# Experts' first pass on 32 rows in four column groups, x gathered in half rows, a fourth home for expert weights

## The chip, the cores and the metric

The kernel runs on one core of a Trainium2 chip. The metric is the device time of one execution in microseconds (us). Times of a kernel are given as the median of several runs; one further execution is profiled, and every duration below comes from that one.

## The reference

Three layers in float32, the last one with float64 weights as inputs:

- Attention over 2 x 8 heads, 768 positions, head width 64: a local window of 16 and block summaries of 32 keys. Its output is x, 1536 rows of 512.
- A mixture of experts with one expert per row and a skip: only rows whose skip score is positive are computed.

```python
do_compute = x @ w_skip > 0
e_idx = np.argmax(xc @ w_gate, axis=1)          # xc: the rows that are computed
for e in range(8):
    h = np.maximum(xc[mask_e] @ w1[e], 0.0)     # 512 -> 1024
    y[mask_e] = gate_w * (h @ w2[e])            # 1024 -> 512
out[do_compute] = xc + y                        # other rows: x as it is
```

- A dense layer on all rows: `h = x @ w_in` (512 to 2048), `g = h * tanh(softplus(h))`, `g @ w_out` (2048 to 512).

Worked through with the reference's own inputs, the routing sends 23, 131, 179, 9, 3, 60, 13 and 10 rows to experts 0 to 7; 1108 rows skip.

## The kernel before

Three stages follow one another on the core. Attention ends at about 100 us of the profiled span, the expert stage runs to about 215 us, and the dense layer fills the rest.

**Routing.** At the end of attention DVE and PE build, per expert, a list of row numbers: `choices` compares each row's rank with `pos` (192 ranks), `pick` turns this by small matmuls into the lists, `id_lists` writes `idl` (half 0: the first 128 ranks, of which 64 are used; half 1: ranks 64 to 191), `counts` writes the number of rows of each expert to `cnti`, and `gate_lists` makes the gate weights. `idle` issues matmuls whose result nobody reads.

**Gathers.** POOL fetches by indirect DMA the first 64 rows of every expert into `xtile[e]` and rows 64 to 191 into three spare tiles `xsb`, 12 gathers one behind the other. All five engines then load nine counts into registers (`load_count`).

**An iteration e of the expert loop.** `g1_pair` multiplies 64 rows by w1[e]: the array is used as two column groups of 64, one for each half of the 1024 hidden columns, 512 moving columns each, over four slices `kk` of the depth. Between the second and the third slice PE transposes the previous expert's hidden layer (`flip`, four blocks of 128), behind the fourth it transposes the next expert's rows (`flip_small`). Then `g2_pair` multiplies the previous expert's hidden layer by w2[e-1], again in two column groups. `If(regs[e] > 64)` runs `whole(e)`, a second pass on 128 more rows with the full array. DVE closes expert e-1 (`close_small`: two passes over 64 x 512), POOL scatters the result to `xd` in DRAM, and DVE converts slices of the dense layer's float64 weights (`go_conv`, six DVE instructions each, ten slices in this stage by `CONVS`).

**Weights.** One expert has 4.19 MB, eight loads of 512 KB on SP's queue. There are three homes: `fwp` for experts 0, 3 and 6, `stg` and `rawp` for 1, 4 and 7, `ring2` for 2 and 5. The first three experts' weights are loaded during attention. Loads of expert e+2 are issued in iteration e, behind `g2_pair(e-1)`, once their home is free. Every engine takes its instructions in the written order (`manual_schedule`).

**Into the dense layer.** Behind the loop come the last `g2_pair`, part of a conversion, the last `close_small` and its scatter. `x_first` loads rows of `xd` back, PE transposes them (`x_turn`, L1313) and the dense layer begins. Its matmuls (L1135, L1384) fill PE to the end.

Of the kernel before, what the change touches and what calls it, by code (L numbers as in the profile page):

```python
# [20 lines left out]
P = 128  # L21
# [7 lines left out]
def kernel(  # L29
# [37 lines left out]
    HT = P // 2  # L67
    CUT = HT + P
# [23 lines left out]
    gtl = const.tile([P, 2, E], F32, name="gtl")  # L92
    tri = const.tile([P, P], BF16, name="tri")
# [74 lines left out]
    def room(key):  # L168
# [5 lines left out]
        if e % 3 == 1:  # L174
            if nm == "w1":
                return stg.tile([P, 2, 512], F32, tag="stg", name="raw")
            return spool[0].tile([P, 2, 512], F32, tag="raw", name="raw")
        if kk % 2 == 0:
            if e % 3 == 0:
                open_[nm] = big((0 if nm == "w1" else 2) + kk // 2)  # L180
            else:
                t = ring2.tile([P, 2, 2, DM], F32R, tag="w2", name="wb")
                open_[nm] = t.rearrange("p a b d -> p (a b) d").bitcast(F32)
# [26 lines left out]
    ring = []  # L210

    make_identity(nc, ident)

    def setup_routing():
# [10 lines left out]
        nc.gpsimd.iota(idp[:, :, 0], pattern=[[P, TT]], base=-IDB, channel_multiplier=0,  # L225
                       allow_small_or_imprecise_dtypes=True)
        nc.gpsimd.iota(idp[:, :, 1], pattern=[[0, TT]], base=0, channel_multiplier=1,
                       allow_small_or_imprecise_dtypes=True)
        nc.gpsimd.iota(pos, pattern=[[1, CUT]], base=0, channel_multiplier=0,
                       allow_small_or_imprecise_dtypes=True)  # L230
        nc.gpsimd.memset(one, 1.0)
# [40 lines left out]
    pos = win.tile([P, CUT], BF16, name="pos")  # L272
# [149 lines left out]
    def idle(lhs, rhs, n, cols):  # L422
        t = ps.tile([P, 512], F32, tag="x", name="idle")[:, 0:cols]
# [168 lines left out]
    def choices(t0, t1):  # L592
        for t in range(t0, t1):
            sels[t] = win.tile([P, CUT], BF16, name=f"sel{t}")
            nc.vector.tensor_scalar(out=sels[t], in0=pos, scalar1=rkf[:, t:t + 1], scalar2=None, op0=ALU.is_equal)
# [10 lines left out]
    def pick(t0, t1, pieces):  # L606
# [3 lines left out]
        mv = mvs.pop((t0, w))  # L610
        lp = ps.tile([P, 2, w, E], F32, tag="tr", name="lp")
        for half in range(2):
            for t in range(t0, t1):
                nc.tensor.matmul(lp[:, half].rearrange("p w e -> p (w e)"), sels[t][:, half * HT:half * HT + P],
# [5 lines left out]
    def id_lists(t0, t1):  # L620
        lpv = pick(t0, t1, idp)
        if t0 == 0:
            nc.vector.tensor_scalar(out=early, in0=lpv, scalar1=float(IDB) / 2, scalar2=None, op0=ALU.add)
        else:
            nc.vector.tensor_tensor(out=early, in0=early, in1=lpv, op=ALU.add)
            nc.vector.tensor_tensor(out=idl, in0=early[:, :, :, 0], in1=early[:, :, :, 1], op=ALU.add)
# [91 lines left out]
    FEED_AT = dict(zip((6, 7, 8, 9, 10, 11, 12, 13, 14, 16, 17, 18, 19, 20), (1, 1, 1, 1, 1, 2, 1, 2, 2, 2, 2, 2, 2, 2)))  # L718
# [201 lines left out]
    id_lists(0, TB)  # L920
# [42 lines left out]
    idle(ident, ident, 2, P)  # L963
# [22 lines left out]
    rows = [ring[0].tile([P, 4, DM], F32, tag="w1", name="xr") for _ in range(E // 4)]  # L986
    xtile = [rows[e // 4][:, e % 4, :] for e in range(E)]
    for t in xtile[:2]:
        nc.gpsimd.memset(t, 0.0)
    for t in (xsb[0], xtile[2], xsb[1], xtile[3], xsb[2], *xtile[4:]):  # L990
        nc.vector.memset(t, 0.0)

    def fetch(idx, t):
        ins = nc.gpsimd.indirect_dma_start(
            out=t, out_offset=None, in_=xd[:, :],
            in_offset=bass.IndirectOffsetOnAxis(ap=idx, axis=0), bounds_check=NT - 1, oob_is_err=False)
# [3 lines left out]
    def store(idx, t):  # L1000
        apart("store", nc.gpsimd.indirect_dma_start(  # L1001
            out=xd[:, :], out_offset=bass.IndirectOffsetOnAxis(ap=idx, axis=0),
            in_=t, in_offset=None, bounds_check=NT - 1, oob_is_err=False), ("store", "fetch"))

    def flip(src, tag):
        pt = mps.tile([P, KD, P], F32, tag=tag, name="pt", bufs=1)
        for c in range(KD):
            nc.tensor.transpose(out=pt[:, c, :], in_=src[:, c * P:(c + 1) * P], identity=ident)  # L1008
        return pt

    def flip_small(src):
        pt = mps.tile([P, KD, HT], F32, tag="xt", name="pt", bufs=1)
        for c in range(KD):
            nc.tensor.transpose(out=pt[:, c, :], in_=src[0:HT, c * P:(c + 1) * P], identity=ident[0:HT, 0:HT])
# [7 lines left out]
    def relu(hp_, tag="hr"):  # L1022
        hr = mo.tile([P, 512], F32, tag=tag, name="hr", bufs=(3 if tag == "hr" else 2))
# [3 lines left out]
    def g1_pair(e, xT, hp_, lo, hi):  # L1027
        for kk in range(lo, hi):
            w = raws["w1", e, kk].rearrange("p a b -> p (a b)")
            for h in range(2):  # L1030
                nc.tensor.matmul(hp_[h * HT:(h + 1) * HT], xT[:, kk, :], w[:, h * 512:(h + 1) * 512],  # L1031
                                 start=(kk == 0), stop=(kk == KD - 1))

    def g2_pair(e, hT, yp, lo=0, hi=KD):
        for c in range(lo, hi):
            for h in range(2):
                nc.tensor.matmul(yp[h * HT:(h + 1) * HT], hT[:, c, h * HT:(h + 1) * HT],  # L1037
                                 raws["w2", e, 2 * h + c // 2][:, c % 2, :], start=(c == 0), stop=(c == KD - 1))
# [467 lines left out]
```

## Time and profile before

| | us |
|---|---|
| median of 3 runs | 507.59 |
| lowest, highest | 506.62, 512.57 |
| profiled execution | 501.91 |
| its span | 500.2 |

The span is the time from the first to the last instruction of the profiled execution; 1.7 us lie around it. In the profile an instruction is named by engine, line and operation, with the tile that it writes and those that it reads. PE is the matrix engine (TensorE), PEld its weight loads, DVE the vector engine, ACT the scalar engine, POOL the engine that issues the gathers, SP the one that issues the other transfers. A float32 matmul shows as two records. A column `x16` counts records. "Landing" is the time from the issue of a transfer until its data is there.

### The profile page before, as it was taken

The numbers are of one execution on the slowest core, as the hardware profiler recorded it, in microseconds if no ns is written. First come the engines' busy times: TensorE is split into PE (matmuls) and PEld (weight loads), VectorE is DVE, ScalarE is ACT, GpSimd is POOL, SyncE is SP. The second block draws the span as 40 slices with busy tenths as digits, with TensorE's granted clock in tenths as the row PEclk, the third lists the DMA queues.
The fourth block names the chain that finished last, engine by engine and source line by source line (L and its number), as shares of the span: only waits on it lengthen the run. The fifth ranks groups of instructions, "written<-read, shape, count | busy, mean of one in ns | idle before, by whom it ended". The sixth has DMA issues, their size and how long they took to land.

```text
span 500.2 us, 8558 instructions
## 1 busy us (share of the span) xinstructions
PE 476.3 (95%) x3262; PEld 365.2 (73%) x3262; DVE 327.8 (66%) x628; ACT 264.5 (53%) x382; POOL 76.5 (15%) x114
## 2 busy tenths in 40 slices
PE   8999998978999999979999999999999999999996
PEld 7777776743434332358989898989898989898985
DVE  4578889740070897634888889887888887453535
ACT  3586772202111121226967778676767676767570
POOL 3368943072020230100000000000000000000000
PEclk9999998959999999999999999999999999999999
DMA  8999999956829399850412121212121000030003
GB/s 202 231 220 245 260 333 354 396 195 229 325 68 370 89 379 397 298 203 12 157 42 86 42 86 42 85 51 76 53 74 54 31 1 2 0 127 0 1 0 126
DMA packets 43695, 74.32 MB, mean 149 GB/s; under 512 B 18863, under 2 KB 18863, under 8 KB 43361
## 3 DMA queue, kind: packets, MB, share of 16 engines
q1 hardware_dynamic: 42080, 71.96, 45.2%
q0 software_dynamic: 1568, 1.76, 1.2%
q8 instruction: 28, 0.46, 0.4%
q14 instruction: 19, 0.15, 0.1%
HBM read 68.80 MB, written 7.86 MB: 153 GB/s over the span
## 4 chain that ended last, share of the span: by engine, by line
PE 54%; DMA 9%; issue 6%; DVE 4%; ACT 2%; POOL 1%; POOLq 0%; DVEq 0%
PE acc L1384 24%; PE hp L1135 23%; DMA xd<-yo,idl 5%; DMA xs<-xd,idl 4%; PE hp L1062 1%; PE yp L1067 1%; PE ptx L1313 1%; PE hp L1031 1%; PE yp L1037 1%; POOL xd L1001 1%; DVE big L1376 1%; DVE big L1365 1%; DMA big<-xd 1%; DVE big L1353 0%; PE pt L1008 0%
## 5 line engine op out<-in xcount | busy, mean ns | idle before, releaser
L1135 PE MATMUL hp<-xt,wi 128*128 128x384 f32 x768 | 140.1, 336 | 2.1 <-ACT xt L1318 1.4
L1135 PEld LDWEIGHTS hp<-xt,wi 128*128 128x128 f32 x768 | 134.5, 188 | 5.3 <-ACT xt L1318 1.9
L1384 PE MATMUL acc<-wo,big 128*128 128x512 f32 x576 | 138.3, 392 | 0.0
L1384 PEld LDWEIGHTS acc<-wo,big 128*128 128x128 f32 x576 | 107.2, 188 | 20.9
L1350 ACT ACTIVATE big<-hp 128x384 f32<-128x384 f32 x64 | 31.3, 492 | 65.7 <-PE hp L1135 65.6
L1365 DVE TENSOR_TENSOR big<-big 128x768 f32<-128x768 f32 x32 | 30.6, 957 | 33.6 <-ACT big L1361 33.6
L1353 DVE COPY big<-hp 128x384 f32<-128x384 f32 x64 | 35.5, 555 | 23.3 <-ACT big L1350 23.3
L1361 ACT ACT_TABLE_LOAD x32 | 41.1, 1283 | 0.6
L1350 ACT ACT_TABLE_LOAD x31 | 39.8, 1283 | 0.6
L1376 DVE TENSOR_TENSOR big<-big 128x768 fp32r<-128x768 f32 x32 | 30.7, 959 | 3.1
L1055 DVE SCALAR_TENSOR_TENSOR yo<-yp,gtl,xs 128x512 f32<-128x512 f32 x2 | 1.5, 752 | 45.8 <-PE yp L1067 45.8
L1361 ACT ACTIVATE big<-big,turn 128x768 f32<-128x768 f32 x32 | 30.0, 939 | 0.4
L370 ACT COPY hT<-pt 128x512 f32<-128x512 f32 x10 | 5.9, 586 | 45.9 <-PE pt L1008 45.9
L1357 ACT ACTIVATE big<-big 128x768 f32<-128x768 f32 x32 | 27.1, 847 | 1.0
L450 DVE TENSOR_REDUCE mx<-sps 128x4 f32<-128x480 f32 x24 | 15.7, 653 | 15.8 <-PE sps L442 15.7
L138 DVE SCALAR_TENSOR_TENSOR cv<-raw,cv 128x512 uint32<-128x512 uint32 x32 | 22.2, 695 | 1.1
L141 DVE SCALAR_TENSOR_TENSOR cv<-raw,cv 128x512 uint32<-128x512 uint32 x32 | 21.9, 684 | 0.3
L1001 POOL DMA_INDIRECT xd<-yo,idl x10 | 10.3, 1030 | 70.8 <-DVE yo L1055 44.5
L1024 ACT ACTIVATE hr<-hp 128x512 f32<-128x512 f32 x12 | 7.2, 598 | 25.9 <-PE hp L1031 15.9
L464 ACT ACTIVATE pts<-tp 120x512 f32<-120x512 f32 x23 | 13.7, 596 | 12.4 <-PE tp L459 11.4
L1373 DVE CAST big<-big 128x768 fp32r<-128x768 f32 x32 | 17.9, 560 | 3.0
L477 PE MATMUL xp<-vw,pts 120*64 120x65 f32 x384 | 17.4, 232 | 2.3 <-issue 1.9
(199 smaller groups left out, 647.8 us busy)
## 6 DMA issues: line engine op xcount, KB each, us to landing
big<-in_moe_w_dram SPq DMA_DIRECT2D x24, 512.0 KB, 7.5
raw<-in_moe_w_dram SPq DMA_DIRECT2D x24, 512.0 KB, 7.0
wb<-in_moe_w_dram SPq DMA_DIRECT2D x16, 512.0 KB, 7.5
raw<-in_moe_w_in_dram SPq DMA_DIRECT2D x16, 512.0 KB, 3.6
raw<-in_moe_w_out_dram SPq DMA_DIRECT2D x16, 512.0 KB, 3.4
kr<-in_k_dram SPq DMA_DIRECT2D x16, 192.0 KB, 4.8
qr<-in_q_dram SPq DMA_DIRECT2D x16, 192.0 KB, 5.3
xd<-xb SPq DMA_DIRECT2D x6, 512.0 KB, 6.8
```

The lines of the kernel that those rows point to most:

```text
L138: nc.vector.scalar_tensor_tensor(out=tu, in0=low, scalar=29, in1=tu, op0=ALU.logical_shift_right, op1=ALU.bitwise_or)
L141: nc.vector.scalar_tensor_tensor(out=tu, in0=high, scalar=0xC0000000, in1=tu, op0=ALU.bitwise_and, op1=ALU.bitwise_or)
L477: nc.tensor.matmul(xv[qs, c, h, :], pt[:, j, qs], vw[:, 4 * g + 2 * c + half, h, VP - D - 1:VP], start=True, stop=True)
L1135: last_up[0] = nc.tensor.matmul(ps_, l(a), r(b_), start=(kk == 0 and n == 0), stop=(kk == KD - 1 and n == 2))
L1350: nc.scalar.activation(out=part(ds[n], half), in_=hps[n, half], func=AF.Sigmoid, scale=-1.0)
L1353: nc.vector.tensor_copy(part(us[n], half), hps.pop((n, half)))
L1357: nc.scalar.activation(out=d, in_=d, func=AF.Arctan)
L1361: nc.scalar.activation(out=d, in_=d, func=AF.Sin, scale=-2.0, bias=turn2)
L1365: nc.vector.tensor_tensor(out=u, in0=u, in1=part(ds[n], half), op=ALU.mult)
L1373: nc.vector.tensor_copy(g_part(n, 0, half), part(us[n], half))
L1376: nc.vector.tensor_tensor(out=g_part(n, 1, half), in0=part(us[n], half), in1=g_part(n, 0, half).bitcast(F32), op=ALU.subtract)
L1384: nc.tensor.matmul(accs[t], g[:, a, t * P:(t + 1) * P], wo[f // 2][:, b_, f % 2, :], start=(n in FIRST and m == 0), stop=(n in LAST and m ...
```

## The change

- The first pass takes 32 rows, not 64. The array is used as four column groups of 32: four groups of 256 hidden columns in the first product (`g1_quad`), two halves of the depth times two halves of the columns in the second (`g2_quad`). A row of x is gathered as two half rows of 256, so that `xtile[e]` is 128 x 256: partitions 0 to 63 hold rows 0 to 31, partitions 64 to 127 rows 32 to 63. `flip` then has two blocks.
- Rows 32 to 63 are a new conditional pass `next_rows` (count over 32), the rest is `whole` as before (count over 64).
- The two halves of the lists are made one after the other, with more `idle` matmuls between; row numbers of half 0 are those of half rows.
- A fourth home: four `ring` tiles, filled with expert 3's weights as soon as the first gathers have landed. Homes are A B C D A B C A. Expert 4's loads are issued in iteration 1, those of 5, 6 and 7 in iterations 2, 3 and 5.
- PE loads expert e's count inside iteration e; the other engines load all nine ahead of the loop.
- Conversions stand ahead of `close_small` (`AHEAD`), between the two conditionals (`BETWEEN`) and at the end of an iteration (`BEHIND`), nine in the loop as before. Two loads of the first three experts' weights move from the attention loop to the remainder behind it (`FEED_AT`).

```diff
-        if e % 3 == 1:
+        home = "ABCDABCA"[e]
+        if home == "B":
...
-    idle(ident, ident, 2, P)
+    idle(ident, ident, 8, P)
...
-    choices(t0, TT)
-    id_lists(t0, TT)
-    idle(ident, ident, 5, P)
+    choices(t0, TT, 0, 1)
+    id_lists(t0, TT, 0)
+    idle(ident, ident, 9, P)
     counts()
+    choices(t0, TT, 1, 2)
+    id_lists(t0, TT, 1)
+    nc.vector.tensor_copy(idn, idl[HT:P, 0, :])
+    idle(ident, ident, 6, P)
     run(rest, 9)
     gate_lists(0, TT)
-    idle(ident, ident, 4, P)
+    idle(ident, ident, 6, P)
...
+    def g1_quad(e, xT, hp_, at, lo, hi):
         for kk in range(lo, hi):
+            n, c = divmod(kk, 2)
             w = raws["w1", e, kk].rearrange("p a b -> p (a b)")
+            for j in range(4):
+                nc.tensor.matmul(hp_[j * TQ:(j + 1) * TQ], xT[:, c, at + n * TQ:at + (n + 1) * TQ],
+                                 w[:, j * HM:(j + 1) * HM], start=(kk == 0), stop=(kk == KD - 1))
+
+    def g2_quad(e, hT, yp, lo=0, hi=2):
+        for i in range(lo, hi):
+            for c in range(2):
+                for h in range(2):
+                    j = 2 * h + i
+                    for n in range(2):
+                        nc.tensor.matmul(yp[(2 * h + n) * TQ:(2 * h + n + 1) * TQ], hT[:, c, j * TQ:(j + 1) * TQ],
+                                         raws["w2", e, j][:, c, n * HM:(n + 1) * HM],
+                                         start=(i == 0 and c == 0), stop=(i == 1 and c == 1))
...
+    def next_rows(e, xT):
+        hp_ = acc_h("hw", HM)
+        g1_quad(e, xT, hp_, HT, 0, KD)
+        hT = drawn(flip(relu(hp_, "yo"), "ht"), "hn", nc.scalar, 3)
+        yp = acc_h("hw", HM)
+        g2_quad(e, hT, yp)
+        close_small(e, yp, HT)
...
+    for nm in ("w1", "w2"):
+        load_expert(3, nm)
+    for eng in engs[1:]:
+        load_counts(range(E + 1), (eng,))
...
+    FOLLOWS = {1: 4, 2: 5, 3: 6, 5: 7}
+    AHEAD = (0, 1, 1, 0, 0, 0, 0, 0)
+    BETWEEN = (0, 2, 2, 0, 0, 0, 0, 0)
+    BEHIND = (0, 0, 0, 1, 1, 0, 1, 0)
...
     for e in range(E):
+        hp_ = acc_h(n=HM)
+        g1_quad(e, xT, hp_, 0, 0, 2)
+        load_counts((e,) if e + 1 < E else (e, E), (ENG.PE,))
         if e:
+            hT = drawn(flip(hr, "ht"), "hn", nc.scalar, 3)
+        g1_quad(e, xT, hp_, 0, 2, KD)
+        hr = relu(hp_, "hq")
+        own_xT = xT
         if e + 1 < E:
+            xT = drawn(flip(xtile[e + 1], "xt"), "xT", nc.scalar)
+        convert(AHEAD[e])
         if e:
+            yp = acc_y(HM)
+            g2_quad(e - 1, hT, yp, 0, 1)
             if e == E - 1:
+                hT_last = drawn(flip(hr, "ht"), "hn", nc.scalar, 3)
+            g2_quad(e - 1, hT, yp, 1, 2)
+            close_small(e - 1, yp)
+            if e in FOLLOWS:
+                for nm in ("w1", "w2"):
+                    load_expert(FOLLOWS[e], nm)
+        if BETWEEN[e]:
+            with tc.If(count(e) > TQ):
+                next_rows(e, own_xT)
+            convert(BETWEEN[e])
+            with tc.If(count(e) > HT):
+                whole(e, spare_of(e))
+        else:
+            with tc.If(count(e) > TQ):
+                next_rows(e, own_xT)
+                with tc.If(count(e) > HT):
+                    whole(e, spare_of(e))
```

## Rows read from the trace of the kernel before

**Rows 1.** The page's 40 equal slices of the span: PE's busy tenths and its granted clock.
```profile
PE   8999998978999999979999999999999999999996
PEclk9999998959999999999999999999999999999999
```

**Rows 2.** Busy time by window: stretch, its length, engines, granted clock, DMA share, GB/s.
```profile
core 0: us, PE busy (x) PEld busy (x) DVE busy (x) ACT busy (x) POOL busy (x), PEclk, DMA share, GB/s
107.40:113.20 5.80, 5.80 (x14) 1.71 (x16) 0.43 (x1) 0.00 (x0) 4.32 (x5) 0.50 1.01 362
123.25:139.40 16.15, 15.47 (x48) 7.21 (x46) 0.00 (x0) 2.95 (x5) 0.00 (x0) 1.00 0.73 261
181.20:189.90 8.70, 8.37 (x40) 2.86 (x40) 7.88 (x15) 1.45 (x3) 2.05 (x2) 1.00 1.03 408
```

**Rows 3.** Timeline of PE over iteration 5: start, duration, line, operation, shape, records, idle before.
```profile
181.24 1.94 PE L1031 MATMUL hp<-wb,xT 128*64 128x512 f32 x8 [0.34 <-DMA wb<-in_moe_w_dram]
183.11 0.66 PE L1008 MATMUL pt<-ident,hr 128*128 128x128 f32 x4
183.69 1.94 PE L1031 MATMUL hp<-wb,xT 128*64 128x512 f32 x8
185.56 0.46 PE L1014 MATMUL pt<-ident,xr 64*128 64x64 f32 x4
185.96 3.65 PE L1037 MATMUL yp<-raw,hT 128*64 128x512 f32 x16
189.95 1.51 PE L1031 MATMUL hp<-big,xT 128*64 128x512 f32 x6 [0.34 <-PEq L1252]
```

**Rows 4.** Timeline of PE in attention: matmuls on 32-column groups and on 64x64 quarters.
```profile
91.63 0.41 PE L512 MATMUL end<-xt,wg 128*32 128x256 f32 x2
91.87 0.39 PE L512 MATMUL end<-xt,wg 128*32 128x256 f32 x2
71.77 0.58 PE L442 MATMUL sps<-kw,qb 64*64 64x120 f32 x16
```

**Rows 5.** Groups of ACT by line and shape, 105 to 216 us: busy, mean ns, idle.
```profile
L1024 ACT ACTIVATE hr<-hp 128x512 f32<-128x512 f32 x12 | 7.2, 598 | 25.9 <-PE hp L1031 15.9 <-PE hp L1062 10.0
L370 ACT COPY xT<-pt 128x256 f32<-128x256 f32 x8 | 2.9, 368 | 10.2 <-PE pt L1014 10.2
```

**Rows 6.** Into the first expert: timelines of DVE and PE, and PE's register loads (ns min/median/max).
```profile
97.03 0.69 PE L425 MATMUL idle<-ident 128*128 128x128 f32 x4
97.63 1.17 DVE L595 TENSOR_SCALAR sel<-pos,rkf 128x192 bf16<-128x192 bf16 x6
101.91 0.81 PE L614 MATMUL lp<-mv,sel 128*128 128x24 bf16 x24 [0.87 <-DVE mv L602]
L1206 PEldq TENSOR_LOAD <-cnti x9: 300/306/495, 102.3 to 105.8; - x9
106.27 0.66 PE L1014 MATMUL pt<-ident,xr 64*128 64x64 f32 x4 [1.65 <-DVE xr L991]
107.39 6.54 PE L1031 MATMUL hp<-big,xT 128*64 128x512 f32 x16 [0.46 <-ACT xT L370]
114.95 0.65 PE L1031 MATMUL hp<-raw,xT 128*64 128x512 f32 x2 [0.62 <-ACTq L1252]
```

**Rows 7.** Gathers issued at 105.10 and 106.35 us: count, us from issue to landing.
```profile
xr<-xd,idl POOLq DMA_INDIRECT x1, 4.9
xs<-xd,idl POOLq DMA_INDIRECT x1, 7.6
```

**Rows 8.** Timelines of DVE, SP and PE from the last iteration into the dense layer.
```profile
208.08 0.74 DVE L1043 SCALAR_TENSOR_TENSOR xr<-yp,gtl,xr 64x512 f32<-64x512 f32 x1 [3.96 <-PE yp L1037]
213.16 0.74 DVE L1043 SCALAR_TENSOR_TENSOR xr<-yp,gtl,xr 64x512 f32<-64x512 f32 x1
217.40 1.31 SPq L1292 DMA_DIRECT2D big<-xd  x3
220.09 0.66 PE L1313 MATMUL ptx<-ident,big 128*128 128x128 f32 x4 [2.33 <-DMA big<-xd]
```

More of the change, by code (lines that the diff above doesn't have):

```diff
@@ L67 @@
     HT = P // 2
+    TQ = P // 4
+    HM = DM // 2
     CUT = HT + P
@@ L609, in pick @@
             spread_(t0, t1, pieces)
-        mv = mvs.pop((t0, w))
-        lp = ps.tile([P, 2, w, E], F32, tag="tr", name="lp")
-        for half in range(2):
+        mv = mvs[t0, w]
+        lp = ps.tile([P, h1 - h0, w, E], F32, tag="tr", name="lp")
+        for half in range(h0, h1):
             for t in range(t0, t1):
-                nc.tensor.matmul(lp[:, half].rearrange("p w e -> p (w e)"), sels[t][:, half * HT:half * HT + P],
+                if t > t0:
+                    idle(ident, ident, stirs, P)
+                nc.tensor.matmul(lp[:, half - h0].rearrange("p w e -> p (w e)"), sels[t][:, half, :],
                                  mv[:, t - t0].rearrange("p w e -> p (w e)"), start=(t == t0), stop=(t == t1 - 1))
@@ L1034, in g2_pair @@
[L1034 to L1038, printed above, removed]
-    def close_small(e, yp):
-        gt, xt = gtl[0:HT, 0, e:e + 1], xtile[e]
-        yo = mo.tile([P, DM], F32, tag="yo", name="yo")[0:HT]
-        nc.vector.scalar_tensor_tensor(out=xt[0:HT], in0=yp[0:HT], scalar=gt, in1=xt[0:HT], op0=ALU.mult, op1=ALU.add)
-        nc.vector.scalar_tensor_tensor(out=yo, in0=yp[HT:P], scalar=gt, in1=xt[0:HT], op0=ALU.mult, op1=ALU.add)
-        store(first_ids(e), yo)
@@ new lines, in close_small, with acc_h @@
+    def close_small(e, yp, at=0):
+        part = slice(at, at + HT)
+        gt, xt = gtl[part, 0, e:e + 1], xtile[e][part]
+        yo = mo.tile([P, DM], F32, tag="yo", name="yo")[0:HT, 0:HM]
+        nc.vector.scalar_tensor_tensor(out=xt, in0=yp[0:HT], scalar=gt, in1=xt, op0=ALU.mult, op1=ALU.add)
+        nc.vector.scalar_tensor_tensor(out=yo, in0=yp[HT:P], scalar=gt, in1=xt, op0=ALU.mult, op1=ALU.add)
+        store((idn if at else idl[0:HT, 0, :])[:, e:e + 1], yo)
+    def acc_h(tag="h", n=512):
+        return mps.tile([P, n], F32, tag=tag, name="hp")
@@ L1217, with load_expert @@
             fetch(idl[:, 1, e - 2:e - 1], spare_of(e - 2))
-        fetch(first_ids(e), xtile[e][0:HT])
-    for e in range(E + 1):
-        load_count(e)
-    xT = drawn(flip_small(xtile[0]), "xT", nc.scalar)
+        fetch(idl[:, 0, e:e + 1], xtile[e])
+    def load_expert(e, nm):
+        for kk in range(KD):
+            load((nm, e, kk))
+    for nm in ("w1", "w2"):
+        load_expert(3, nm)
+    for eng in engs[1:]:
+        load_counts(range(E + 1), (eng,))
+    xT = drawn(flip(xtile[0], "xt"), "xT", nc.scalar)
@@ L1238 @@
             if e == E - 1:
-                hT = drawn(flip(hr, "ht"), "hT", nc.scalar), hT
-                g2_pair(e - 1, hT[1], yp, 2, KD)
-                hT = hT[0]
-            else:
-                g2_pair(e - 1, hT, yp, 2, KD)
-            if e + 2 < E:
-                for kk in range(KD):
-                    load(("w1", e + 2, kk))
-            while len(SEQ) - len(queue) < min(EARLY, done + NCVR):
-                load_next()
-            if e + 2 < E:
-                for kk in range(KD):
-                    load(("w2", e + 2, kk))
@@ L1256 @@
         if e == E - 1:
-            with tc.If(regs[E] > CUT):
+            with tc.If(count(E) > CUT):
                 enroll()
```

145 lines of the change are left out of this document (78 added, 67 removed).

## Prediction

> **What bounds the kernel now.** I began with the page's slices: PE is busy nine tenths or more nearly everywhere, and the granted clock is far down in one slice only, from 100 to 112.5 us [rows 1]. Then I took the windows by stage. An expert without a second pass keeps PE busy for 8.37 of 8.70 us while DMA moves 408 GB/s; expert 1's second pass keeps it busy for 15.47 of 16.15 us [rows 2]. So PE sets the length of the expert stage, with DMA close behind in places. Third, the timeline of one iteration shows what PE does in it: 4.0 us of first product, 1.0 of transposes, 3.65 of second product and 0.34 of branch, 8.71 us from 181.24 to 189.95 [rows 3]. Fourth, the way into the stage: PE idles 1.65 us ahead of 106.27, and expert 0's first product takes 6.54 us at half the clock [rows 2, 6]. Last, the tail: behind the last products DVE converts and closes, a scatter and a load follow, and PE's next work of the dense layer begins at 220.09 [rows 8]. The dense layer is PE's own and nothing of it is edited, so what the stage gains comes off the end.
>
> **The first pass.** The second product has 16 records in pairs: 8 steps and a first latency in 3.65 us, so a step is 0.43 us and the rest 0.2 [rows 3]. Two groups of 64 columns thus run at the same time. With four groups of 32 and 256 moving columns, a step is four records of half the length. Does a quad run at the same time too? Two rows come near it. Groups of 32 with 256 columns: the first records of two groups begin together at 91.63, their second ones 0.24 us later [rows 4]. Four 64x64 quarters of 120 columns: 16 records in 0.58 us, that is four steps of 0.1 and 0.2 of latency [rows 4]. In series a quad would take 0.86. I take half of the pair step, 0.215, with 0.24 as the slow bound. The first product is then 8 steps of 0.215 where it was 8 of 0.43 in two halves of 1.87 us: each half 1.01. The hidden layer has two blocks to transpose instead of four: 0.58 becomes 0.37. The rows have two blocks of 128 where they had four of 64, no change at 0.40 to 0.37. The second product with its latency and the branch goes from 3.99 to 2.27. An iteration takes 5.03, 3.69 us less.
>
> [...]
>
> **Behind the quads.** The transposed hidden layer is drawn by ACT in an estimated 0.37 us, as the 256-column copy is [rows 5]; PE has 1.4 us of other work before it needs it. ACT and DVE get smaller tiles throughout. PE's count load (0.31 us, [rows 6]) sits behind four steps of matmuls already queued, 0.86 us, and I cost it at nothing; uncovered it would be 0.3 x 8 = 2.4 us.
>
> **Rows 32 to 63.** The reference's counts send experts 1, 2 and 5 into `next_rows`. It has no other work between its steps: product 1.87, relu 0.37 and 0.06 to PE, transposes 0.37, copy 0.37 and 0.06, product 1.87 with latency, and 0.3 for the hand-overs to ACT: 5.26 us. Three times: +15.8 us. `whole` for experts 1 and 2 stays 16.15 [rows 2]. Its second accumulator waits for DVE's close of `next_rows`, which has 4.8 us for it.
>
> **Iteration by iteration.** Expert 0: 107.39 to 114.95 is 7.56 us before [rows 6]. At the full clock I expect 1.87 of product, then transposes, relu and copy in series, 0.88: 2.75, so -4.81. Expert 1: -3.69 + 5.26, and a wait for its gather (below) of 1.3: +2.87. Expert 2: +1.57. Experts 3 and 4: -3.69 each. Expert 5: +1.57. Expert 6: -3.69. Expert 7 has another transpose of the hidden layer: -3.69 - 0.21. Together -13.8.
>
> **The start.** An `idle` matmul costs 0.215 (two records of 128 columns, a quarter of two 0.43 steps). Eight of them from 97.03 hold PE until 98.75, the picks of half 0 with five more between until 100.0. Before, the picks went with DVE's comparisons, which end at 98.8 [rows 6]. So the first list and the first gathers come about 1 us later, and nothing waits for them before 106.9. DVE then has the counts, half 1's comparisons, its list and a copy ahead of the gate chain: 10 instructions of about 0.2 us [rows 6] and a round trip to PE, an estimated 3 us. The picks of the gate lists, at 101.91 before [rows 6], go to 104.9 and end at 105.7; six `idle` make 1.3 us, and PE transposes expert 0's rows at 106.9 instead of 106.27. PE's nine count loads, 102.3 to 106.1 [rows 6], which held it those 1.65 us, are no longer ahead of it. With the copy, the first product begins at 107.8: +0.4. In exchange PE has matmuls almost all the way from 97 to 107. It lost the clock around 100 behind a stretch of small matmuls and few others [rows 1, 6] and had it back only after the 5.80 us of expert 0 [rows 2]. I take it as held; that is in the 4.81.
>
> The tiles of the later gathers are cleared by DVE behind the gate lists, so now 3 us later. Expert 2's gather is issued near 108.1, with twelve 512 KB loads on the queue instead of four. Gathers landed 4.9 and 7.6 us after issue with four [rows 7]: 113.0 to 115.7. PE wants it at 113.3: a wait of 0 to 2.4, and I take 1.3. Others have tens of us.
>
> **DMA.** At 408 GB/s [rows 2] an expert is 10.3 us. Expert 3 is on the queue near 106, landed by 125, due at 164. Expert 4: issued at 116, due at 169. Expert 5: 142, due at 174. Expert 6: 168, landed 179, due at 184. Expert 7 waits for expert 4's home at 178.5, queues behind 6: w1 at 184.5, due 189; w2 at 189.5, due 194. Slack 4.5 us: nothing. The two shifted early loads keep their volume ahead of 100 us, and the attention rows go out sooner: nothing.
>
> **The tail.** The last second product gets shorter, but DVE decides: from the first close at 208.08 to the last at 213.16 lie two closing passes and 3.4 us of conversion [rows 8]. A pass of 0.74 on 256 columns is an estimated 0.46, by the ratio of ACT's rows [rows 5]. That takes 0.55 off each close: -1.1. Scatter, landing and load (to 220.09) stay at 5.4.
>
> **The sum.** -13.8 + 0.4 - 1.1 = -14.5 us. On the profiled execution that is 501.91 - 14.5 = 487.4; it lies 5.7 below the median of the runs, so on the median 507.59 - 14.5 = 493.
>
> **The rivals.**
> - Quads overlap in part. Each 0.01 us of a step counts 176 times (11 passes of 16): at the 0.24 of [rows 4] the time is 497.5; were the 0.025 there the price of three groups, a quad would take 0.25, and the time is 499. Against: that is a first step, which holds some latency. Chance 0.12. [...]
> - The clock is lost on the way in or at the gather's wait. Array work of expert 0, expert 1's first pass and `next_rows` is about 9.4 us and would take twice that: up to 502, half of it 498. For it: the drop before, and a stretch with little PE work around 105. Chance 0.14.
> - Expert 6's or 7's weights come late: if loads run at 300 GB/s, 7 us more for the two against 4.5 of slack: 496. Chance 0.06.
> - Slower: the clock lost near 105 stays at half through expert 1's second pass. That adds 15 us to the 9.4: 493 + 24.4 = 517. From 14.5 us of array work at half the gain is gone, from 25 the kernel is slower by 2%. Against: the uninterrupted 5.80 us of [rows 2] sufficed to bring it back, and the second pass has such stretches. Chance 0.05.
> - The change does not do what it says (the stage is paced elsewhere, by DVE's conversions of 4 us each): the stage keeps its length, 505. PE's 8.37 of 8.70 speaks against it [rows 2]. Chance 0.03.
>
> **How the numbers follow.** The forecast case has 0.60: 493, own range 489 to 497 (the wait 0 to 2.4, the step, the count loads). The low end is 487: the runs after may lie as low beside their median as the profiled one did. The high end takes in the partial overlap and most of the clock case: 502. About 2 in 10 are outside. Two per cent, about what a measurement of this kernel can tell from no change, is 497.4: faster 0.57 of the forecast, 0.07 of the clock case, 0.04 of the rest, 0.68; slower than 517.7 only the long half clock, 0.05; the same 0.27.
>
> **What would show it.** Iterations 3, 4 and 6 at 5.0 us; second products of 32 records in about 1.9 us; `next_rows` near 5.3, three times; clock 1.00 from 97 us on; first product at 107.8, the dense layer's first transposes near 205.6. [...]

## The result: about as fast as before, 17 us short of the sum

The changed kernel takes 510.07 us in the median (505.99 to 513.42); the runs of the kernel before beside it have a median of 506.79. The ratio is 1.0069, 95% interval 1.0046 to 1.0091: within 2%, and a little slower. I had forecast 493.

The profiled execution of the changed kernel has a span of 510.4 us, that of the kernel before 500.2. The two differ by more than the medians do: attention ended 2.8 us later in this execution, and over all traces of this study its last gate matmul lies anywhere from 88.5 to 97.1 us, whichever kernel it is. So I compare stages by their lengths. From the first product to the first transposes of the dense layer the kernel before takes 112.70 us (107.39 to 220.09, [rows 6, 8]; 112.99 in a second trace), the changed one 118.51 (111.61 to 230.12; 118.51 in a second trace). My sum had 97.8. The dense layer has not changed (280.1 and 280.3 us).

Of the page of the changed kernel, PE's busy tenths, its granted clock, and the two queues on which code is fetched:

```profile
PE   8997998973898968687999999999999999999996
PEclk9999999995999998889999999999999999999999
...
q8 instruction: 35, 0.57, 0.5%
q14 instruction: 21, 0.17, 0.1%
```

Against [rows 1] PE has new hollows in the tenth, the fifteenth and the seventeenth slice, with a lower clock in or behind them. Queue q8 brings TensorE's code: 35 blocks of 16 KB (0.57 MB) where the page of the kernel before has 28. (The third and the sixth experiment lengthen TensorE's code alone, and q8 then has 31 and 38.)

The work itself runs as worked out. Timeline of PE over iterations 3 and 4 (start, duration, records):

```profile
176.21 1.07 PE L1062 MATMUL hp<-wb,xT 128*32 128x256 f32 x16
177.22 0.44 PE L1044 MATMUL pt<-ident,hr 128*128 128x128 f32 x2
177.59 1.07 PE L1062 MATMUL hp<-wb,xT 128*32 128x256 f32 x16
178.59 0.44 PE L1044 MATMUL pt<-ident,xq 128*128 128x128 f32 x2
178.96 1.93 PE L1071 MATMUL yp<-wb,hn 128*32 128x256 f32 x32
181.24 1.07 PE L1062 MATMUL hp<-big,xT 128*32 128x256 f32 x16 [0.35 <-PEq L1323]
...
183.98 1.93 PE L1071 MATMUL yp<-wb,hn 128*32 128x256 f32 x32
190.31 1.29 PE L1062 MATMUL hp<-raw,xT 128*32 128x256 f32 x16 [4.39 <-PEq L1323]
191.53 0.69 PE L1044 MATMUL pt<-ident,hr 128*128 128x128 f32 x2
192.15 1.94 PE L1062 MATMUL hp<-raw,xT 128*32 128x256 f32 x16
```

Iteration 3 takes 5.03 us (176.21 to 181.24) where [rows 3] had 8.71, and the second product of 32 records 1.93. But behind expert 4's branch PE stands still for 4.39 us, and the products after it run at about half their speed (16 records in 1.94 us, 1.07 before). What PE waited for from 104 to 235 us, in us, times, longest:

```profile
PE hp L1062 <- remote: 8.7, 1, 8.7
PE hp L1062 <- PEq L1323: 4.7, 2, 4.4
PE hp L1062 <- issue: 3.5, 1, 3.5
PE lp L631 <- DVE mv L617: 1.5, 1, 1.5
PE hp L1106 <- ACT xw L381: 1.5, 2, 0.7
PE yp L1071 <- DVEq L1323: 1.4, 1, 1.4
PE yp L1071 <- issue: 1.3, 2, 1.0
```

The stalls are 8.70 us in expert 0 (113.92 to 122.62), 4.39 behind expert 4's branch, 3.48 inside expert 7's first product (208.43 to 211.91), and 1.38 and 1.04 around the last product: 19 us. What the 8.70 are is still open at the end; the experiments explain the others, but for the 1.38. The clock by stretch (engines' busy us, then granted clock, DMA share and GB/s):

```profile
116.00:120.00 4.00, 0.00 (x0) 0.00 (x0) 1.94 (x4) 0.00 (x0) 3.08 (x4) 0.50 1.01 363
120.00:124.00 4.00, 1.38 (x16) 0.60 (x16) 0.00 (x0) 0.76 (x2) 2.92 (x3) 0.50 1.04 395
...
186.00:191.00 5.00, 0.69 (x15) 0.50 (x16) 4.54 (x9) 0.00 (x0) 1.71 (x2) 1.00 0.60 216
191.00:196.00 5.00, 5.00 (x56) 2.10 (x52) 0.69 (x1) 1.13 (x3) 0.41 (x1) 0.66 0.86 307
```

The clock fell to 0.50 within the first long stall and about the ends of the two others, and stayed there for 10, 3.4 and 3.4 us; it fell once more behind the stalls around the last product, from 222 to 225 us. Iteration 5 lost 1.5 us by that: 4.26 us from 190.31 to its second product, 2.74 in iteration 4.

PE's branch at expert 4 took 5.51 us, and one block of code arrived within it. This is the row of PE's branches behind the expert loop's `If` (ns, min/median/max), and below it the DMA packets and the code queue from 184 to 190 us (packets, MB, share):

```profile
L1323 PEldq COMPARE_BRANCH  x6: 70/397/5512, 112.4 to 216.9; - x6
...
DMA packets 936, 1.63 MB, mean 271 GB/s; under 512 B 169, under 2 KB 169, under 8 KB 935
...
q8 instruction: 1, 0.02, 1.0%
```

### The profile page after: what moved, and what is told of

It is laid out like the page before. It is cut to its first block, busy times and chain, and to the rows that moved or that the text cites. A ratio compares the mean times of both kernels' runs of the same rounds, so it can differ in the third digit from the quotient of the medians.

```text
span 510.4 us, 9590 instructions
## 1 busy us (share of the span) xinstructions
PE 468.5 (92%) x3730; PEld 373.6 (73%) x3730; DVE 326.0 (64%) x644; ACT 263.9 (52%) x388; POOL 79.9 (16%) x121
## 4 chain that ended last, share of the span: by engine, by line
PE 48%; DVE 4%; ACT 2%; DMA 1%; issue 1%; another core or an unknown queue 0%; POOLq 0%; SPq 0%; DVEq 0%
PE acc L1452 24%; PE hp L1179 23%; PE ptx L1381 1%; DMA big<-xd 1%; DVE big L1444 1%; DVE big L1433 1%; DMA xd<-yo,idl 0%; DVE xt L1387 0%; DVE big L1421 0%; ACT big L1429 0%; DVE big L1441 0%; ACT big L1425 0%; DVE wo L120 0%; DVE cv L142 0%; ACT big L1418 0%
## 5 line engine op out<-in xcount | busy, mean ns | idle before, releaser
L1054 ACT ACTIVATE hr<-hp 128x256 f32<-128x256 f32 (+1 forms) x15 | 6.6, 441 | 36.9 <-PE hp L1062 12.7
L1079 DVE SCALAR_TENSOR_TENSOR xq<-yp,gtl,xq 64x256 f32<-64x256 f32 x8 | 3.8, 475 | 33.0 <-PE yp L1071 33.0
L381 ACT COPY hn<-pt 128x256 f32<-128x256 f32 x11 | 4.1, 373 | 39.5 <-PE pt L1044 33.0
L1062 PE MATMUL hp<-raw,xT 128*32 128x256 f32 x128 | 10.6, 469 | 13.1 <-remote 8.7
```

## The theories

- **A, code.** The block that is skipped grew from some 90 TensorE instructions (`whole`) to some 230 (`next_rows` and `whole`), counted in the compiled programs, while an iteration fell from 8.7 to 5.0 us. (The records of the traces give nearly the same: `whole` shows 44 matmul and 44 weight-load records, `next_rows` 66 and 66.) PE comes to code that is not loaded yet, and its fetch goes over the same DMA engines as the weights (the page counts q8 on the same 16 engines, with 0.5% of their span).
- **B, data.** Gathers or weights land late behind the twelve loads ahead of the loop.
- **C, the start.** The late end of attention and the longer way to the first product cost the time.

All ratios below are to the kernel before, run on the same chip beside them, with the 95% interval.

## Experiment 1: no bodies that are never entered

```diff
-        else:
+        elif e == 5:
             with tc.If(count(e) > TQ):
                 next_rows(e, own_xT)
-                with tc.If(count(e) > HT):
-                    whole(e, spare_of(e))
```

> The changed kernel without the conditional bodies that this input never enters: experts 0, 3, 4, 6 and 7 have no rows 32 to 63 pass and no whole second pass, expert 5 no whole second pass (their counts, 23, 179 and so on, are the input's; what is left out is never run here). Everything that is run stays. Theory A (the stalls are code: behind a skipped body the instructions of the target are not loaded and their fetch queues behind the weight loads): the PE idle times of 8.70, 4.39, 3.48, 1.38 and 1.04 us go, the clock stays at 1.00 through the experts, time 487 to 494 us, ratio to before 0.96 to 0.975. Theory B (the stalls are data: gathers and weights that land late behind the twelve loads ahead of the loop): nothing that is run has changed, so the stalls stay and the time is 506 to 512 us. Theory C (the start, 2.8 us later at the end of attention and 1.4 us more to the first product, is what costs): 506 to 512 us too.

488.78 us, ratio 0.9715 (0.9648 to 0.9782). Timeline of PE over iterations 3 to 5, and what PE waited for:

```profile
163.69 1.07 PE L1062 MATMUL hp<-wb,xT 128*32 128x256 f32 x16
...
168.17 1.05 PE L1062 MATMUL hp<-big,xT 128*32 128x256 f32 x16
...
172.64 1.05 PE L1062 MATMUL hp<-raw,xT 128*32 128x256 f32 x16
```

```profile
PE ptx L1379 <- DMA big<-xd: 3.8, 1, 3.8
PE pt L1044 <- ACT hr L1054: 3.3, 3, 2.3
PE pt L1044 <- DMA xq<-xd,idl: 2.7, 1, 2.7
```

An iteration is 4.48 us, the stalls behind branches are gone, and the expert stage takes 99.15 us. Nothing that this input runs was removed but the branches, on all five engines. B and C fall as the main cause: the missing time is in skipping. By the two ratios (1.0069 and 0.9715) it is 3.5% of the kernel, 18 us, but the first of them belongs to a run that had the 8.70 us of expert 0. The next experiment's kernel (the changed one but for the place of expert 3's loads), which ran on the same chip as this one without that wait, takes 14.7 us more than this one (503.46 and 488.78), 3%. Of these, 2.7 are the five branches themselves, 0.55 us for each iteration (5.03 against 4.48).

One thing expected did not come: the clock does not stay at 1.00 (its mean over the span is 0.991). In expert 5's `next_rows` PE waits 2.3 us for ACT's relu, 0.7 in the changed kernel, and the product behind it takes 3.07 us, where the one of as many records at 166.42 takes 1.93. Why isn't known.

## Experiments 2 to 4: loads, and the length of a skip

Expert 3's loads in iteration 0 instead of ahead of the loop:

```diff
-    for nm in ("w1", "w2"):
-        load_expert(3, nm)
...
+        if e == 0:
+            for nm in ("w1", "w2"):
+                load_expert(3, nm)
```

> The changed kernel with the eight loads of expert 3 issued in iteration 0, behind its branch's issue place, in place of ahead of the loop. Theory A: the fetch at expert 0's branch finds fewer weights ahead of it, so the 8.70 us falls to 1 to 4 us; the later stalls (4.39 and 3.48 us) stay; 501 to 506 us. Theory B: the 8.70 us falls as well, and what ended it was a landing, so expert 3's own iteration may wait for its weights instead; 503 to 510 us. Theory C: 508 to 511 us.

Ratio 1.0014 (0.9977 to 1.0051). The gap in expert 0 was 2.8 us, on a gather (`xq<-xd,idl`). But the fourth experiment, which ran on the same chip with the loads where the change has them, shows 2.5 us there, so this edit did not bring it. The 4.1 and 4.0 us at experts 4 and 7 stand.

The kernel before, with 32 matmuls more in the body that experts 0 and 3 to 7 never enter:

```diff
-        g1(ha, 0, 0, KD)
+        for _ in range(pad + 1):
+            g1(ha, 0, 0, KD)
...
-            whole(e, spare_of(e))
+            whole(e, spare_of(e), 0 if e in (1, 2) else 8)
```

> The kernel before with a longer body in the conditional whole pass of experts 0 and 3 to 7, which this input never enters: 32 more matmuls that are never run, so that the skipped TensorE code is about 230 instructions as in the changed kernel, in place of about 100. Nothing that is run changes. Theory A: stalls of 1 to 9 us appear on PE behind the skipped branches, with clock lost after them, 511 to 527 us, ratio 1.01 to 1.04. Theories B and C: no code that runs has changed, 505 to 508 us, ratio 0.998 to 1.002.

Ratio 1.0022 (0.9990 to 1.0053): theory A as I had written it is wrong here. A skip of 220 instructions alone costs nothing that can be measured in iterations of 8.7 us. PE's branches (ns, min/median/max) show one long one, at expert 7, of which 1.2 us was PE's idle time:

```profile
L1253 PEldq COMPARE_BRANCH  x10: 70/265/3836, 106.8 to 203.0; - x10
```

Two skips in place of one in the changed kernel:

```diff
                 next_rows(e, own_xT)
-                with tc.If(count(e) > HT):
-                    whole(e, spare_of(e))
+            with tc.If(count(e) > HT):
+                whole(e, spare_of(e))
```

> The changed kernel with the whole second pass behind the rows 32 to 63 pass as a block of its own, not nested, for experts 0 and 3 to 7: two skips of about 125 and 100 TensorE instructions one behind the other in place of one skip of about 230. Theory A in the form that one jump must not be longer than what is loaded ahead: the stalls go but for some 0.3 us for each further branch, 490 to 497 us. Theory A in the form that the code stands behind the weights however it is skipped: 506 to 513 us. Theories B and C: 509 to 513 us (five more branches of 0.3 us).

Ratio 1.0019 (0.9982 to 1.0055). The stalls stand at the same places (4.46, 4.23 and 2.97 us at experts 4 and 7 and the last product). So in these iterations it is not how far one jump reaches that counts, but how much code is passed.

## Experiments 5 to 8: how much code in how much time

The changed kernel, with an instruction on TensorE's queue that names each skip's target ahead:

```diff
+        if not BETWEEN[e]:
+            tc.mark_branch_hint_location(f"more{e}", "LikelyTaken", [ENG.PE])
...
-            with tc.If(count(e) > TQ):
+            with tc.If(count(e) > TQ, label=f"more{e}"):
```

> The changed kernel with one more instruction on TensorE's queue at the start of iterations 0 and 3 to 7, which names the target of that iteration's skip beforehand so that its code can be fetched in time; every body and branch stays. Theory A (the stalls are the fetch of code that the skip lands on): the fetch is under way some 2 to 5 us before the branch, so the 4 us stall behind expert 4's branch falls below 1 us, and the one inside expert 7's first product, which stands behind a skip too, shrinks or goes; 490 to 500 us, ratio 0.97 to 0.99. Theory B (data that lands late): as the changed kernel, ratio 1.00 to 1.01. Theory C (the start): ratio 1.00 to 1.01.

Ratio 1.0051 (1.0009 to 1.0092). In the compiled program all six of these instructions stood at the start of the program, so the run says nothing about hints; expert 4's branch took 6.05 us.

The kernel before with a skip of 509 instructions (the third experiment's edit with 26 in place of 8):

> The kernel before with 104 matmuls that are never run in the conditional pass of experts 0 and 3 to 7, so that each skip passes over some 520 TensorE instructions (33 KB). Theory A: whatever was loaded ahead in order, a skip of this length lands behind it, so each of the six skipped branches of PE takes 3 to 6 us where it took 0.2 to 0.4: 515 to 535 us, ratio 1.02 to 1.065. Theories B and C: no instruction that runs has changed, ratio 0.998 to 1.003.

523.83 us, ratio 1.0296 (1.0225 to 1.0367), with no instruction more that runs. PE's branches, as above, of this kernel and of the kernel before in a second trace:

```profile
L1253 PEldq COMPARE_BRANCH  x10: 70/3726/7302, 104.2 to 220.8; - x10
```

```profile
L1252 PEldq COMPARE_BRANCH  x10: 70/254/358, 105.2 to 202.6; - x10
```

Every one of the six skips became long (3.6 to 7.3 us). This shows the cost of skipped code in the kernel before too, with none of the change's data or order, and with code added on TensorE alone.

The changed kernel once more:

> The changed kernel once more. If the 8.70 us of iteration 0 is of every execution, the profile shows it again and the first product starts near 111.6 us; if it belongs to the one execution profiled, the gap is below 3 us, as in the two experiments with the same code there, and the stalls of some 4 us behind expert 4's branch and inside expert 7's first product stand at the same places. Ratio 1.004 to 1.010 under all theories.

Ratio 1.0061 (1.0021 to 1.0100). Its first waits of PE:

```profile
PE hp L1062 <- ACTq L1323: 9.0, 1, 9.0
PE hp L1062 <- DMA wb<-in_moe_w_dram: 4.3, 1, 4.3
PE hp L1062 <- issue: 3.2, 1, 3.2
```

The same three stalls at the same places. The 4.3 us are put down to a load here, but PE's branch at expert 4 lasts 5.45 us, and a block of code comes within it; the row names whatever landed last.

The skips shortened to some 100 instructions, by leaving `next_rows` out where it is never entered:

```diff
             with tc.If(count(e) > TQ):
-                next_rows(e, own_xT)
+                if e == 5:
+                    next_rows(e, own_xT)
```

> The changed kernel with the rows 32 to 63 pass left out of the conditional block of experts 0, 3, 4, 6 and 7, which this input never enters, so that these skips pass over some 100 TensorE instructions (6.4 KB) as in the kernel before, in place of some 230. Theory A in the form that what counts is how much code an iteration of 5 us moves through: 18 KB in place of 26 KB, so one of the two 4 us stalls goes or both shrink; 492 to 501 us, ratio 0.98 to 0.997. Theory A in the form that any skip of a fast iteration stalls: ratio 1.00 to 1.01. Theories B and C: ratio 1.00 to 1.01.

502.33 us, ratio 0.9905 (0.9865 to 0.9944). What PE waited for from 165 to 222 us:

```profile
PE hp L1062 <- issue: 1.7, 1, 1.7
PE yp L1071 <- DVEq L1323: 1.4, 1, 1.4
...
PE hp L1062 <- PEq L1323: 0.7, 2, 0.3
```

Behind expert 4's branch PE waits 0.3 us in place of 4.39, inside expert 7's first product 1.7 in place of 3.48. The 1.4 us ahead of the last product, put down to DVE's queue, stay as they were, so they don't go by the length of the skip.

Skipped code is fetched too. By the counts of the table below, the kernel before with the long skips passes 6 x 129 TensorE instructions more that are never run, the one with two blocks 6 x 418. Their pages show 31 and 38 blocks, 3 and 10 more than that of the kernel before, so a block holds some 250 instructions (774 by 3, 2508 by 10):

```profile
q8 instruction: 31, 0.51, 0.4%
```

```profile
q8 instruction: 38, 0.62, 0.5%
```

Without the bodies the changed kernel's page has 30 blocks in place of 35, with the whole pass only 32.

Put together, per iteration with a skip (instructions counted in the compiled programs, 250 taken as a block):

| kernel | run + skipped | us per iteration | us per block | PE's stalls for code, experts 3 to 7 and the last product (us) |
|---|---|---|---|---|
| before | 87 + 91 | 8.7 | 12.2 | none over 0.4 |
| no bodies (first experiment) | 141 + 0 | 4.5 | 8.0 | none |
| before, long skip (third) | 87 + 220 | 8.7 | 7.1 | 1.2 |
| whole pass only | 144 + 98 | 5.0 | 5.2 | 1.7 |
| before, two blocks | 87 + 509 | 8.7 | 3.6 | 8.0, 2.7, 3.7 |
| after | 144 + 230 | 5.0 | 3.3 | 4.4, 3.5, 1.0 |

A block that was needed and not there took 5.8 us, from the branch at 184.48 to PE's next matmul at 190.31. The rows with clearly more than that per block (12.2 and 8.0 us) have no stall for code, those with clearly less (3.6 and 3.3) have long ones, and the two near it (7.1 and 5.2) short ones. PE doesn't wait in every iteration; which of them it spares, and why, no run singles out.

The traces go with A in this form: 16 KB packets on q8, some 250 instructions in each, no branch of PE over 0.4 us in the kernel before, six of 3.6 to 7.3 us in the one whose skips pass two blocks. A wait for code comes in straight code too, 3.48 us in expert 7's first product just behind a skip: in the changed kernel's trace a block starts on q8 at 209.3, within that wait, and PE goes on 2.6 us later, at 211.91.

## Experiments 9 to 14: the fetch behind the weights, and a better kernel

The kernel before again, and the hint in its place on the queue:

```diff
+    def name_target(label):
+        tc.mark_branch_hint_location(label, "LikelyTaken", [ENG.PE])
+        *_, last, mark = (i for i in nc.cur_bb.bb.instructions if i.engine == ENG.PE)
+        tc.add_manual_dep(mark, last.name, ...)
...
+        g1_quad(e, xT, hp_, 0, 0, 1)
+        if not BETWEEN[e]:
+            name_target(f"more{e}")
+        g1_quad(e, xT, hp_, 0, 1, 2)
```

> The kernel before, unchanged, for a second trace of it. Theory A makes the stalls by the code that an iteration moves past: here 93 TensorE instructions are skipped and some 87 run in 8.7 us, so no PE idle time over 1 us stands behind the skipped branches of experts 3 to 7. A long PE idle time in expert 0 (8.7, 9.0 and 9.1 us in three profiles of kernels with the change, 2.5 to 2.8 us in three others) is open: if it shows here too, the change does not make it. Ratio 1.

> The changed kernel with the instruction that names the skip's target standing in its place on TensorE's queue, behind the first four column groups of iterations 0 and 3 to 7 and so some 120 instructions ahead of each branch (in the earlier run with it the instructions had been moved to the start of the program, where they do nothing). Theory A: the fetch of the target starts some 3 us ahead of the branch, beside that of the code next in order; the two stalls of some 4 us shrink below 2 us each; 494 to 503 us, ratio 0.98 to 0.997. If the chip takes the hint but fetches one block after the other, ratio 0.995 to 1.005. Theory B (data) and theory C (start): ratio 1.002 to 1.010.

Before again: ratio 0.9984 (0.9951 to 1.0017), its longest branch of PE 0.358 us (the row above). With the hints in place, one some 120 instructions ahead of each branch: 1.0077 (1.0041 to 1.0113). Expert 4's branch took 5.66 us, its block left at 178.06, 3.3 us behind the branch, much as without the hint (3.1). Naming the target did not start a fetch here; why not stays open.

The changed kernel without the loads of experts 4 to 7:

```diff
-                    load_expert(FOLLOWS[e], nm)
+                    for kk in range(KD):
+                        raws[nm, FOLLOWS[e], kk] = raws[nm, {4: 0, 5: 1, 6: 2, 7: 0}[FOLLOWS[e]], kk]
```

> The changed kernel without the loads of the weights of experts 4 to 7 (32 transfers of 512 KB are left out; their matmuls read the weights of an earlier expert in the same home, so the output is not the reference's). The DMA engines are then nearly free from about 150 us on. Theory A with the fetch queueing behind the weights: each fetch is shorter, the 5.5 us at expert 4's branch falls to 2.5 to 4 us and the stall in expert 7's first product shrinks too, ratio to before 0.985 to 1.0. Theory A with a fetch that takes its time on an idle memory as well: the stalls stay at 4 us, ratio 1.00 to 1.007. Theory B (data that lands late): no weights are left that could be late, so both stalls go altogether, ratio 0.97 to 0.985.

Ratio 0.9905 (0.9867 to 0.9943). Two stalls of one execution, with the DMA around each (timeline of PE, then busy time, clock, DMA share and GB/s by stretch):

```profile
176.39 1.07 PE L1062 MATMUL hp<-raw,xT 128*32 128x256 f32 x16 [1.14 <-PEq L1324]
...
196.16 1.25 PE L1062 MATMUL hp<-big,xT 128*32 128x256 f32 x9 [4.08 <-issue]
```

```profile
174.00:178.00 4.00, 2.86 (x46) 1.37 (x42) 3.53 (x7) 0.07 (x1) 1.54 (x2) 1.00 0.02 4
...
190.00:194.00 4.00, 1.90 (x31) 0.70 (x23) 2.35 (x5) 0.00 (x0) 1.07 (x1) 1.00 0.92 324
```

At expert 4 the DMA engines were free (busy share 0.02), and the branch took 2.43 us (173.79), with 1.14 of idle PE. At expert 7 the dense layer's first loads kept them at 0.92, and PE waited 4.08. The same kind of fetch takes 2.6 us from branch to matmul on free engines and 5.8 behind loads. This is what A with a queue says, and B not: a stall of 4 us stands where no expert's weights are on the way. It is one execution, and the traces further below bear it out.

One late skip in place of three. The bodies of experts 6 and 7, whose weights stay in place to the end, go into one block with the rare pass; a count that this block needs is made beside the others:

```diff
+        nc.vector.tensor_scalar(out=rest_, in0=mc, scalar1=float(TQ - CUT), scalar2=None, op0=ALU.add)
+        for d in (6, 7):
+            nc.vector.tensor_tensor(out=rest_, in0=rest_, in1=cntf[:, d:d + 1], op=ALU.max)
...
-        else:
+        elif e < 6:
...
+            with tc.If(count(E + 1) > TQ):
+                for d in (6, 7):
+                    with tc.If(count(d) > TQ):
+                        next_rows(d, drawn(flip(xtile[d], "xt"), "xT", nc.scalar), True)
+                        with tc.If(count(d) > HT):
+                            whole(d, spare_of(d))
+                with tc.If(count(E) > CUT):
...
-    BEHIND = (0, 0, 0, 1, 1, 0, 1, 0)
+    BEHIND = (0, 0, 0, 1, 1, 0, 0, 1)
```

> The changed kernel with the conditional bodies of experts 6 and 7 moved into one outer block in front of the last product, together with the rare pass, so that one skip there takes the place of three (a further count, the largest of what exceeds, decides; for any input the same rows are computed; one conversion is moved behind it, too). Theory A: iterations 6 and 7 move through 144 TensorE instructions each in place of some 374, so the 3 to 4 us in expert 7's first product go, the 4.4 us behind expert 4's branch stay, and the one long skip at the end costs 3 to 6 us in place of 2 to 3: ratio to before 0.990 to 1.002. Theory B and C: as the changed kernel, 1.002 to 1.010.

497.15 us, ratio 0.9927 (0.9898 to 0.9956). What PE waited for:

```profile
PE hp L1068 <- PEq L1329: 4.7, 2, 4.4
PE pt L1050 <- DMA xq<-xd,idl: 4.3, 1, 4.3
PE yp L1077 <- PEq L1338: 2.6, 1, 2.6
```

Expert 7's stall is gone, expert 4's stands at 4.38, and the long skip costs 2.6 where the three places had 3.5, 1.4 and 1.0. By its conditions it computes the same rows for any input (this input is the only one that was run), and it is faster than the kernel before, by 0.7%; the changed kernel's ratios were 1.0061 and 1.0069.

Last, expert 6's loads behind expert 4's block, alone and with the late skip:

```diff
-    FOLLOWS = {1: 4, 2: 5, 3: 6, 5: 7}
+    FOLLOWS = {1: 4, 2: 5, 5: 7}
...
+        if e == 4:
+            for nm in ("w1", "w2"):
+                load_expert(6, nm)
```

> The changed kernel with the eight loads of expert 6 issued behind expert 4's conditional block in place of behind expert 3's product; all else as changed. Theory A with the code fetch queueing behind the weights: the fetch at expert 4's branch finds the DMA engines free, as in the run without the late loads (2.43 us there against 5.45 to 5.66 us with them), so the 4.3 us of PE idle time fall to 1 to 1.5 us and the half clock behind them goes; the stall in expert 7's first product stays; ratio to before 0.993 to 1.003. If the fetch takes its time whatever else moves: 1.002 to 1.009, with the 4.3 us in place. If expert 6's weights then come late: a wait of PE on wb in iteration 6 of 1 to 4 us, 1.000 to 1.008.

> Both at once: the bodies of experts 6 and 7 in one outer block at the end, and the loads of expert 6 behind expert 4's block. Theory A: the two savings add, about 3 us and half a microsecond to two of clock below the run with the one late skip (0.9927): ratio to before 0.982 to 0.989, 491 to 496 us where before takes 501. If the stalls were one cause that moves on to the next place: 0.990 to 0.996.

Alone 1.0072 (1.0043 to 1.0101), together 0.9931 (0.9901 to 0.9961). Neither ratio is in the range that theory A had given it, and the ratio of the first shows no gain. Yet in its trace, expert 4's stall is shorter, though not 1 to 1.5 us, and the clock still fell behind it. Here are SP's loads of experts 6 and 7, and what PE waited for behind that branch (2.27 us):

```profile
161.69 12.13 SPq L207 DMA_DIRECT2D wb<-in_moe_w_dram  x8
178.58 8.27 SPq L207 DMA_DIRECT2D big<-in_moe_w_dram  x8
```

```profile
PE hp L1062 <- DMA wb<-in_moe_w_dram: 2.3, 1, 2.3
```

SP is well ahead of PE, so a place behind PE's branch is no later for it: the eight loads went out by 174, before the branch at 175.02, and the DMA engines were busy for 0.85 of the time from 175 to 176. So the edit did not free them as it was meant to. With both edits the stall is back at 4.28 us, and the ratio repeats that of the late skip alone. That ratio lies where it was expected if the stalls were one cause that moves on to the next place, but expert 4's stall had not gone, so it says nothing for that.

Where the stall's length comes from can be read in four of the traces, at expert 4's branch, from the moment at which the block of code starts on q8 (all in us):

| run | branch | block starts | next matmul | branch to block | block to matmul |
|---|---|---|---|---|---|
| no late loads | 173.79 | 173.85 | 176.39 | 0.06 | 2.54 |
| expert 6's loads later | 175.02 | 176.04 | 178.75 | 1.02 | 2.71 |
| changed kernel | 184.48 | 187.57 | 190.31 | 3.09 | 2.74 |
| hint in place | 174.81 | 178.06 | 180.79 | 3.25 | 2.73 |

Once a block has started, PE goes on some 2.5 to 2.7 us later in each of them. What differs is how long the block waits to start: 0.06 us on free DMA engines, 1 to 3.3 us while the weights are on the way. In none of the four does it start ahead of the branch.

## Why the prediction was wrong

**Right.** The quads: 0.215 us a step, 1.93 for the second product, an iteration of 5.03. `next_rows` 5.4, 5.2 and 5.4 us, forecast 5.26. `whole` unchanged. No wait for late weights. And the sum itself: without the bodies that are skipped the ratio is 0.9715, and 493 on 507.59 is 0.9713. That it meets so well is partly luck: the run also lacks the branches, 0.55 us for each iteration, and on the other side the start and the gather's wait cost more than I had.

**The step that failed** is the branch. I had "The second product with its latency and the branch goes from 3.99 to 2.27", with the 0.34 us of [rows 3] for a skip, and nothing for the code that is skipped. Those 0.34 us were the price of a skip of 91 instructions in 8.7 us. The change made both worse: more code to pass, less time to fetch it in. The term that the sum put at nothing is some 12 us: the 14.7 us between two kernels on one chip, with and without the bodies, less 2.7 for the branches themselves. The profiled execution has nearly the same: stalls of 4.39, 3.48 and 1.04 us, and by the slower products behind them an estimated 4 us at half the clock. The other 8.70 us of stall there, in expert 0, are not shown to be code.

**The gather's wait.** I took 1.3 us, with 2.4 as the most. In the eight traces of kernels with the change that don't have the long wait in expert 0, PE waits 2.5 to 4.3 us for the rows of `xq`. This term was too small by 1.2 to 3 us, and the wait is over the most that I had allowed.

**The clock.** I took it as held and had its loss as a rival. It was held into the first product (1.00 from 97 to 114 us), where I had looked, and was lost behind each long stall, where I had not. That is a consequence; without the bodies the mean clock is 0.991 (0.978 in the profiled execution of the changed kernel).

**The start.** From the last gate matmul to the first product it takes 16.95 us, 15.5 before; I had +0.4 and it is +1.4 (+1.0 in six other traces of kernels with the change). The gate lists' picks wait 1.54 us for DVE's `mv`, which the longer work on the lists delays: the round trip that I put at 3 us was short by about one.

**DMA slack "nothing".** True for the weights, but the loads delay the code: 2.6 us from branch to matmul became 5.8.

**The rival that came nearest in time**, that the stage keeps its length (505), was not it. PE was not paced by DVE; it was held by its own instruction stream, which I had no rival for.

**Open.** The 8.7 to 9.1 us in expert 0. Three profiles of kernels with the change have it, one has 5.9, the others 2.5 to 4.3 of waiting for a gather. ACT's relu and PE's next work wait there together. In the two traces of the changed kernel a block of code arrives within the wait, but 5 to 6 us ahead of its end; with the skips shortened to some 100 instructions the wait is as long (9.1 us), and no block arrives in it. So the length of the skip alone does not make it. Part of the trace's semaphore records of that stretch are missing in just these profiles. The three whose chip is on record (5.9, 9.0 and 9.1 us) come from one chip, and the eight traces from four other chips don't have it. Two traces of the kernel before don't show it either, but none was kept that is known to be from that chip. Whether it is the chip, the tracing or the change isn't settled.

## What to carry to other kernels

Count the instructions that a branch passes, not only its own time: divide what an iteration runs and skips by some 250, and compare the time per block with a fetch, which took 2.6 us on free DMA engines here and 5.8 behind weight loads. A change that splits matmuls into more, shorter ones makes the code longer and the time for its fetch shorter at once (here 178 instructions in 8.7 us became 374 in 5.0). Bodies that are seldom entered belong together behind one skip, where the data that they need stays in place (ratio 0.9927 here, against 1.0061 and 1.0069).

## What the runs showed of the hardware

- Code that is only skipped costs: 509 instructions in place of 91, never run, in each of six skips made the kernel 2.96% slower.
- Skipped code is fetched all the same, a block of 16 KB for each 250 instructions or so: 28 blocks became 31 and 38 with code that never runs.
- At expert 4's branch the missing block of code started on its queue only once the branch had begun, in four traces, and PE went on 2.5 to 2.7 us later. Beside weight loads it first waited 1 to 3.3 us, without them 0.06.
- A stall for code need not stand at the branch. Expert 7's, 3.48 us in the changed kernel, stood several matmuls behind it, marked "issue" (nothing that the profile shows); a block of code started on its queue 0.8 us into it.
- An instruction that names a branch's target ahead did not bring its code sooner: expert 4's branch took 5.66 us with it and 5.45 without.
